# RWKV-5 attention into a SiLU layer pair: the loads, state copies and weight requests of the first eight units in another order

## The chip, the cores and the metric

The kernel runs on one core of one Trainium2 chip. A core has five engines with a queue each: TensorE (PE) for matrix products, VectorE (DVE), ScalarE (ACT) and GpSimd (POOL) for work on tiles, and SyncE (SP), which here only starts DMA transfers. ACT and POOL start transfers too. The engines run side by side and wait for each other by semaphores; within one queue the order is that of the program. The metric is device microseconds of one execution, as the median of five runs.

## The reference

The input of two matrix products with a SiLU between them is the output of a linear attention with a decaying state.

```python
batch, n_heads, seq, head_dim = (4, 8, 768, 48)
...
for t in range(S):
    cur = np.einsum('bhd,bhe->bhde', u[None] * kt, vt)
    y[:, :, t] = np.einsum('bhd,bhde->bhe', rt, state + cur)
    state = w[None, :, :, None] * state + np.einsum('bhd,bhe->bhde', kt, vt)
...
x = np.ascontiguousarray(attn_out.transpose(0, 2, 1, 3)).reshape(B * S, H * D)
h = x @ w_in          # 384 -> 2048
g = h * (1.0 / (1.0 + np.exp(-h)))
out = g @ w_out       # 2048 -> 384
```

r, k and v are fp32 of 4 x 8 x 768 x 48; the output is 3072 x 384.

## The kernel before

**Tiling.** The sequence is cut into six chunks of 128 steps. One chunk of one batch entry, all eight heads, is a *unit*; unit i has chunk i // 4 and batch entry i % 4, so there are 24. Units 0 to 3 are chunk 0 and have no earlier state.

**One unit** passes these steps; the two-letter words are those of the order string in the code.
- Loads `lr lk lv` of r, k, v (192 KB each, on SP's queue unless said otherwise; line 73).
- `T`: PE transposes r and k, in fp32, into one of two PSUM buffers called att (242). `rT kT`: DVE multiplies them by powers of the decay w, lamR and lamK (248). `A`: PE forms the 128 x 128 products of each head (270; for units from 4 on two units together, 283). `am`: DVE masks them to fp16 (290).
- The bonus term: `ku` (k times u, 202) and `ru` (times r, 206) on POOL, `rd`, a sum over the head's columns, on DVE (215), `vu` (that sum times v, 220) on POOL.
- `v16`: ACT casts v to fp16 (229; for odd units from 5 on two half copies more, 232 and 233). `r16`: ACT casts rT (263), needed when there is a state.
- `Y`: PE forms the outputs from am and v16, and from the state when there is one (300, 305). `y16`: DVE adds vu (333). `yT` and `xT`: PE transposes, ACT copies the result to the second layer's input (371, 375). From unit 6 on a DMA transposes instead (364).
- The state: `kc` (k times decay, POOL, 210), `S` (PE, 317), `sd` (old state times w to the 128th, POOL, 328), `st` (new state into SBUF, 344), `stb` (its fp16 copy, POOL, 353). In chunk 0 there is no old state, and `st` writes the fp16 copy (347) and the fp32 state (348) itself, each in two parts of 48 partitions.

**The layer pair.** `L` is a piece of the first product: two blocks of 128 hidden columns for two batch entries (386); `G` its SiLU on ACT (394). `L0.f` is for batch entries 0 and 1, `L2.f` for 2 and 3, f the first block. `H0` to `H3` do both for chunk 1. The second product is ops (407). The weights come in four parts each, `i_q0` to `i_q3` for w_in (84) and `i_o0` to `i_o3` for w_out (89), started from POOL and cast to fp16 on the way. Part n of w_in serves the blocks 4n to 4n + 3.

**PSUM.** y, yT, the state products, L's output and ops all take turns in one ring of four buffers with the tag `moe`; a new use waits until the use four turns earlier has been read.

**Order.** The work of units 0 to 5 and the first part of 6 and 7 is written out by hand in the order string: an instruction goes to the end of its engine's queue in the order of the words. `n*` ahead of a word puts n matmuls without use (`spin`, 157) on PE. After the string a loop handles two units at a time; pieces of the two layers are put between its steps by `fill`. In the loop's first turn (units 6 and 7) the bonus sums come behind both masks.

The setup ahead of the order string starts the loads of units 0 to 3, small loads of w and the load of u to all partitions (u_bc, 192 KB, line 105, on ACT's queue). v of unit 0 and k of unit 1 go by ACT's queue.

Of the kernel before, what the change touches and what calls it, by code (L numbers as in the profile page):

```python
# [15 lines left out]
def kernel(  # L16
# [11 lines left out]
    nc = tc.nc  # L28

    B, H, S, D = r.shape  # L30
    C = 128
    NCH = S // C
    HD = H * D
# [16 lines left out]
    def unit(i):  # L50
        return divmod(i, B)
# [10 lines left out]
    rin = [big.tile([128, H, 64], FP, name=f"rin{i}") for i in range(NIN)]  # L62
    kin = [big.tile([128, H, 64], FP, name=f"kin{i}") for i in range(NIN)]
    vin = [big.tile([128, H, D], FP, name=f"vin{i}") for i in range(NIN)]
    kc = [big.tile([128, H, 64], F16, name=f"kc{i}") for i in range(NIN)]
    st = [big.tile([PR, NP, PW], FP, name=f"st{b}") for b in range(B)]
    st16 = [big.tile([PR, NP, PW], F16, name=f"stb{b}") for b in range(B)]
# [3 lines left out]
    def ld(i, dst, src, eng=nc.sync):  # L71
        sc, b = unit(i)
        eng.dma_start(
            out=dst[i % NIN][:, :, 0:D],
            in_=src[b, :, sc * C:sc * C + C, :].rearrange("h t d -> t h d"))

    def load(i):
        if i >= NU:
            return
        for dst, src in ((rin, r), (kin, k), (vin, v)):  # L80
            ld(i, dst, src)
# [11 lines left out]
    def columns(eng, dst, src, j):  # L93
        eng.dma_start(out=dst[64 * j:64 * j + D, :],
                      in_=bass.AP(tensor=src.tensor, offset=D * j, ap=[[1, D], [PW, NP]]))

    w_row = cst.tile([1, HD], FP)
# [4 lines left out]
    nc.vector.memset(idle, 0.0)  # L102
    columns(nc.sync, wpT, w, 1)
    columns(nc.scalar, wpT, w, 0)
    nc.scalar.dma_start(out=u_bc, in_=bass.AP(tensor=u.tensor, offset=0,
                                              ap=[[0, 128], [D, H], [1, D]]))
    nc.scalar.dma_start(out=w_row, in_=bass.AP(tensor=w.tensor, offset=0, ap=[[0, 1], [1, HD]]))
    for i in range(B):
        for dst, src in ((rin, r), (kin, k), (vin, v)):
            by_act = (i == 0 and dst is vin) or (i == 1 and dst is kin)  # L110
            ld(i, dst, src, nc.scalar if by_act else nc.sync)
    nc.vector.memset(ones, 1.0)
    for i in range(B):
        nc.vector.memset(rin[i][:, :, D:64], 0.0)
# [1 line left out]
    for b in range(B):  # L116
# [13 lines left out]
        out=maskM, in_=maskM, compare_op=ALU.is_ge, fill=0.0,  # L130
# [10 lines left out]
    eK = cst.tile([PR, NP, C], FP)  # L141
    lamR = cst.tile([PR, NP, C], FP)
    lamK = cst.tile([PR, NP, C], FP)
    lnw_bc = cst.tile([128, HD], FP)
    lamC = cst.tile([128, H, D], FP)
# [47 lines left out]
    def L(i):  # L193
        return live.setdefault(i, {})

    def bonus_products(i):
        bonus_ku(i)
        bonus_rku(i)
# [10 lines left out]
    def decayed_k(i):  # L209
        nc.gpsimd.tensor_tensor(out=kc[i % NIN][:, :, 0:D], in0=kin[i % NIN][:, :, 0:D],  # L210
                                in1=lamC, op=ALU.mult)

    def bonus_sum(i):
        L(i)["rku"] = wrk.tile([128, H], FP, name="rku")
        nc.vector.tensor_reduce(out=L(i)["rku"], in_=L(i)["rku_f"],  # L215
                                axis=mybir.AxisListType.X, op=ALU.add)

    def bonus_v(i):
        L(i)["vu"] = wrk.tile([128, H, D], FP, name="vu")
        nc.gpsimd.tensor_tensor(out=L(i)["vu"], in0=vin[i % NIN],  # L220
                                in1=L(i)["rku"].unsqueeze(2).broadcast_to([128, H, D]),
                                op=ALU.mult)

    def crossed(i):
        return i >= B and i % 2 == 1
# [47 lines left out]
    def product_pair(i):  # L273
        a = [next_att().rearrange("p j (g c) -> p j g c", g=NP) for _ in range(2)]
        for e in range(2):
            L(i + e)["a"] = a[e]
        for s0, c0 in ((0, 0), (HC, HC)):
            for p in range(NP):
                for e in range(2):
                    rT, kT = L(i + e)["rT"], L(i + e)["kT"]  # L280
                    o0 = s0 if e == 0 else HC - s0
                    for j, r0 in ((0, 0), (1, 64)):
                        nc.tensor.matmul(a[e][o0:o0 + HC, j, p, c0:C],  # L283
                                         kT[r0:r0 + D, p, s0:s0 + HC],
                                         rT[r0:r0 + D, p, c0:C],
                                         start=True, stop=True)

    def masked(i):
        am = L(i)["am"] = wrk.tile([128, 2, NP, C], F16, name="am")
        nc.vector.tensor_tensor(  # L290
            out=am.rearrange("p h g c -> p (h g) c"), in0=L(i)["a"].rearrange("p h g c -> p (h g) c"),
            in1=(maskX if crossed(i) else maskM).unsqueeze(1).broadcast_to([128, H, C]), op=ALU.mult)
# [27 lines left out]
    def outputs(i):  # L320
        outputs_y(i)
        outputs_s(i)

    def decayed_state(i):
        sc, b = unit(i)
        if 0 < sc < NCH - 1:
            L(i)["sdec"] = wrk.tile([PR, NP, PW], FP, name="sdec", bufs=4)
            nc.gpsimd.tensor_tensor(out=L(i)["sdec"], in0=st[b],  # L328
                                    in1=wCT.unsqueeze(2).broadcast_to([PR, NP, PW]), op=ALU.mult)

    def evict_y(i):
        L(i)["y16"] = wrk.tile([128, H, D], F16, name="y16")
        nc.vector.tensor_tensor(out=L(i)["y16"], in0=L(i)["y"], in1=L(i)["vu"], op=ALU.add)  # L333

    def state(i):
        sc, b = unit(i)
        if sc == NCH - 1:
            return
        sps = L(i)["sps"]
        for p0, c0 in ((0, 0), (64, D)):  # L340
            dst = st[b][p0:p0 + D, :, c0:c0 + D]
            src = sps[p0:p0 + D, :, c0:c0 + D]
            if sc:
                nc.vector.tensor_tensor(out=dst, in0=src,
                                        in1=L(i)["sdec"][p0:p0 + D, :, c0:c0 + D], op=ALU.add)
            else:
                nc.scalar.copy(out=st16[b][p0:p0 + D, :, c0:c0 + D], in_=src)  # L347
                nc.scalar.copy(out=dst, in_=src)

    def state16(i):  # L350
        sc, b = unit(i)
# [74 lines left out]
    def fill(n):  # L426
        for _ in range(n):
            if fillers:
                fillers.pop(0)()
# [7 lines left out]
    def first(sc):  # L437
        return [lambda f=f: l1(sc, 0, B, f) for f in range(NFT)]
# [5 lines left out]
    def piece(word, f):  # L444
# [16 lines left out]
        "lr": lambda i: ld(i, rin, r), "lk": lambda i: ld(i, kin, k), "lv": lambda i: ld(i, vin, v),  # L461
    }
    order = """
        lnw eK lamK pads lr4 lk4 lv4 lr5 lk5 lv5 lr6 lk6 lv6 lr7 lk7 lv7 10*T0 ku0 kT0 rT0 v160
        ru0 5*A0 rd0 ku1 am0 T1 wb v161 ru1 lnwb lamC kT1 rT1 1*Y0 vu0 rd1 T2 i_q0 y160 A1 vu1
        yT0 xT0 v162 ku2 am1 kT2 rT2 ru2 4*Y1 y161 2*A2 yT1 xT1 i_q1 rd2 vu2 v163 T3 am2 ku3 kT3
        rT3 Y2 L0.0 y162 ru3 A3 i_q2 L0.2 G0.0 yT2 G0.2 xT2 rd3 am3 vu3 kc0 Y3 L0.4 G0.4 y163
        kc1 L0.6 G0.6 yT3 kc2 S0 st0 xT3 i_q3 kc3 L2.0 G2.0 L2.2 G2.2 S1 st1 L2.4 G2.4 L2.6 G2.6
        ku4 mx S2 st2 L0.8 G0.8 L0.10 G0.10 S3 st3 ru4 T4 kT4 rT4 v164 r164 L2.8 G2.8 L2.10
        G2.10 rd4 ku5 i_o0 vu4 T5 kT5 rT5 r165 v165 A45 ru5 kc4 sd4 L0.12 G0.12 am4 L0.14 G0.14  # L470
        am5 kc5 rd5 vu5 sd5 Y4 S4 y164 L2.12 G2.12 st4 Y5 S5 y165 L2.14 G2.14 st5 yT4 xT4 stb4
        stb5 i_o1 T6 kT6 rT6 yT5 xT5 ku6 ru6 i_o2 kc6 v166 r166 H0 H1 H2 T7 kT7 rT7 i_o3 H3 r167
        v167 ku7 ru7 kc7 sd6 sd7
    """
    for word in order.split():
        if "*" in word:
            n, word = word.split("*")
# [18 lines left out]
    for i in range(B + 2, NU, 2):  # L496
        sc, b = unit(i)
        nxt = range(i + 2, min(i + 4, NU))
        product_pair(i)
        if i > B + 2:  # L500
            for n in nxt:
                bonus_products(n)
                decayed_k(n)
        masked(i)
        masked(i + 1)
        if i == B + 2:
            for n in (i, i + 1):
                bonus_sum(n)
                bonus_v(n)
            for n in nxt:  # L510
                bonus_products(n)
                decayed_k(n)
        fill(4)
        outputs(i)
        evict_y(i)
        turn_y_dma(i)
        state(i)
        state16(i)
        fill(2)
        outputs(i + 1)  # L520
        evict_y(i + 1)
        turn_y_dma(i + 1)
        state(i + 1)
        state16(i + 1)
        if b:
            fillers.extend((first(sc) if sc > 1 else rest_first(sc)) + second(sc))
        fill(2)
        for n in nxt:
            turn(n)
            decay(n)  # L530
        load(i + B)
        load(i + 1 + B)
        for n in nxt:
            bonus_sum(n)
            cast_v(n)
            bonus_v(n)
            decayed_state(n)
        for n in nxt:
            fill(2)
            cast_r(n)  # L540
        fill(4)
# [31 lines left out]
```

## Time and profile before

| | |
|---|---|
| median of 5 runs | 197.89 us (197.85 to 198.14) |
| the profiled execution | 198.1 us, of which the span is 196.4 us |
| busy share of the span | PE 94%, weight loads 61%, DVE 50%, ACT 56%, POOL 61% |
| the chain that ended last | PE 76%, ACT 6%, DVE 6%, POOL 4%, DMA 4% |
| first product (386), PE | 384 matmuls, 67.7 us |
| second product (407), PE | 384 matmuls, 66.4 us |
| SiLU (394), ACT | 96 instructions, 55.4 us, mean 598 ns |
| `stb` and `st` of chunk 0 (347, 348), ACT | 16 instructions, 314 ns and 313 ns in the median |
| `ku`, `ru`, `kc` (202, 206, 210), POOL | 24 each, about 1000 ns each |
| `vu` (220), POOL | 24, 829 ns |
| w_in and w_out parts, request to landing | 6.3 and 5.7 us in the median |
| r, k, v, request to landing | 3.9, 3.8 and 4.0 us in the median |

The span is the time from the first instruction of the program to the last; the time of a run also holds what lies around it. Times within the span are told in us from its start. A share of busy time is an average over the whole span, which here has two parts: about 56 us in which the first units are worked off and the layer pair begins, and the rest, a regular loop.

### The profile page before, as it was taken

The page shows a single profiled execution, that of the slowest core. Times are in us where ns is not written, and L with a number is a line of the kernel's source. Part 1 is how long each engine was busy: PE and PEld are TensorE (multiplying, and loading weights), DVE is VectorE, ACT ScalarE, POOL GpSimd, SP SyncE. Part 2 cuts the span into 40 slices and gives each one's busy share as a digit, 9 for nine tenths or more (in the row PEclk, how much of TensorE's full clock was granted, in tenths as well). Part 3 has the DMA queues.
Part 4 walks back from the last instruction along what each step waited for, and adds up shares of the span by engine and source line. Part 5 has one row for each costly group of instructions (what it writes and reads, how often), then busy time and mean ns, then how long its engine had stood idle before and what let it go on. Part 6 is the DMA issues. An engine that isn't in the chain of part 4 may idle for free.

```text
span 196.4 us, 5505 instructions
## 1 busy us (share of the span) xinstructions
PE 183.8 (94%) x2250; PEld 120.3 (61%) x2250; DVE 97.9 (50%) x172; ACT 109.9 (56%) x223; POOL 120.4 (61%) x159
## 2 busy tenths in 40 slices
PE   7897868789989999999999999999999999999992
PEld 2465757667756787665556665556755657644561
DVE  6389503683682772782782673664564355100121
ACT  4672579968553286056794076792286781089200
POOL 8698993779999958919919829839739130000000
PEclk9999999999999999999999999999999999999998
DMA  4999999899939549259149268177286101410022
GB/s 73 249 181 207 216 201 171 157 191 128 133 78 193 173 84 197 92 125 218 38 84 216 67 152 193 23 142 163 74 183 150 40 3 40 120 43 0 0 80 80
DMA packets 90122, 24.33 MB, mean 124 GB/s; under 512 B 83313, under 2 KB 90098, under 8 KB 90098
## 3 DMA queue, kind: packets, MB, share of 16 engines
q1 hardware_dynamic: 83952, 20.26, 47.3%
q0 software_dynamic: 3712, 3.15, 11.5%
q10 hardware_dynamic: 2434, 0.59, 1.5%
q8 instruction: 17, 0.28, 0.6%
q14 instruction: 7, 0.06, 0.1%
HBM read 20.65 MB, written 4.72 MB: 129 GB/s over the span
## 4 chain that ended last, share of the span: by engine, by line
PE 76%; ACT 6%; DVE 6%; POOL 4%; DMA 4%; issue 2%; SPq 0%; POOLq 0%; DVEq 0%
PE ops L407 32%; PE hps L386 26%; PE att L283 6%; PE att L242 5%; PE att L270 2%; DVE am L290 2%; ACT gT L394 2%; DMA rin<-in_r_dram 2%; PE yp L305 2%; DMA vin<-in_v_dram 2%; PE yp L300 1%; PE sp L317 1%; DVE rT L248 1%; DVE kT L248 1%; ACT stb L347 1%
## 5 line engine op out<-in xcount | busy, mean ns | idle before, releaser
L386 PE MATMUL hps<-xT,win 128*128 128x256 f16 (+1 forms) x384 | 67.7, 326 | 3.0 <-ACT xT L375 2.4
L407 PE MATMUL ops<-wout,gT 128*128 128x384 f16 x384 | 66.4, 326 | 0.0
L394 ACT ACTIVATE gT<-hps 128x512 f16<-128x512 f32 x96 | 55.4, 598 | 18.2 <-PE hps L386 15.9
L386 PEld LDWEIGHTS <-win 128*128 128x128 f16 x384 | 35.8, 98 | 25.4 <-issue 3.2
L407 PEld LDWEIGHTS <-gT 128*128 128x128 f16 x384 | 36.2, 98 | 23.3
L220 POOL TENSOR_TENSOR vu<-vin,rku 128x384 f32<-128x384 f32 x24 | 19.8, 829 | 31.6 <-DVE rku L215 28.3
L413 ACT COPY osb<-ops 128x384 f32<-128x384 f32 x20 | 9.6, 480 | 45.1 <-PE ops L407 45.1
L290 DVE TENSOR_TENSOR am<-att,maskM 128x1024 f16<-128x1024 f32 x14 | 17.2, 1225 | 35.1 <-PE att L283 33.5
L202 POOL TENSOR_TENSOR ku<-kin,u_bc 128x384 f32<-128x384 f32 x24 | 24.1, 1003 | 1.8 <-DMA kin<-in_k_dram 1.6
L206 POOL TENSOR_TENSOR rku_f<-rin,ku 128x384 f32<-128x384 f32 x24 | 24.1, 1003 | 1.8
L210 POOL TENSOR_TENSOR kc<-kin,lamC 128x384 f16<-128x384 f32 x24 | 24.0, 1001 | 0.0
L248 DVE TENSOR_TENSOR kT<-att,lamK 112x512 f32<-112x512 f32 x24 | 16.4, 683 | 14.0 <-PE att L242 14.0
L333 DVE TENSOR_TENSOR y<-yp,vu 128x384 f16<-128x384 f32 x24 | 13.3, 556 | 14.9 <-POOL ku L202 4.5
L248 DVE TENSOR_TENSOR rT<-att,lamR 112x512 f32<-112x512 f32 x24 | 16.4, 685 | 7.2 <-ACT gT L394 4.0
L283 PE MATMUL att<-rT,kT 48*64 48x128 f32 (+1 forms) x640 | 16.5, 248 | 1.3 <-DVE rT L248 1.3
L283 PEld LDWEIGHTS att<-rT,kT 48*64 48x64 f32 x640 | 14.7, 133 | 4.9 <-issue 3.1
L415 DVE COPY osb<-ops 128x384 f32<-128x384 f32 x4 | 2.2, 558 | 22.4 <-PE ops L407 22.4
L328 POOL TENSOR_TENSOR sdec<-st,wCT 112x384 f32<-112x384 f32 x16 | 13.2, 827 | 0.0
L229 ACT CAST v<-vin 128x384 f16<-128x384 f32 x24 | 11.5, 512 | 2.2 <-DMA vin<-in_v_dram 2.1
L263 ACT CAST rT<-rT 112x512 f16<-112x512 f32 x20 | 12.5, 623 | 0.4 <-DVE rT L248 0.3
L215 DVE TENSOR_REDUCE rku<-rku_f 128x8 f32<-128x384 f32 x24 | 12.3, 544 | 0.1
L290 DVE TENSOR_TENSOR am<-att,maskX 128x1024 f16<-128x1024 f32 x10 | 12.2, 1215 | 0.0
(60 smaller groups left out, 168.6 us busy)
## 6 DMA issues: line engine op xcount, KB each, us to landing
rin<-in_r_dram SPq DMA_DIRECT2D x24, 192.0 KB, 3.9
out_dram<-osb SPq DMA_DIRECT2D x24, 192.0 KB, 2.1
kin<-in_k_dram SPq DMA_DIRECT2D x23, 192.0 KB, 3.8
vin<-in_v_dram SPq DMA_DIRECT2D x23, 192.0 KB, 4.0
win<-in_moe_w_in_dram POOLq DMA_DIRECT2D x4, 384.0 KB, 6.3
wout<-in_moe_w_out_dram POOLq DMA_DIRECT2D x4, 384.0 KB, 5.7
xT<-y SPq DMA_TRANSPOSE x18, 2.3
u_bc<-in_u_dram ACTq DMA_DIRECT2D x1, 192.0 KB, 4.0
```

The costliest lines, as they stand in the source:

```text
L202: nc.gpsimd.tensor_tensor(out=L(i)["ku"], in0=kin[i % NIN][:, :, 0:D], in1=u_bc, op=ALU.mult)
L206: nc.gpsimd.tensor_tensor(out=L(i)["rku_f"], in0=rin[i % NIN][:, :, 0:D], in1=L(i)["ku"], op=ALU.mult)
L210: nc.gpsimd.tensor_tensor(out=kc[i % NIN][:, :, 0:D], in0=kin[i % NIN][:, :, 0:D], in1=lamC, op=ALU.mult)
L220: nc.gpsimd.tensor_tensor(out=L(i)["vu"], in0=vin[i % NIN], in1=L(i)["rku"].unsqueeze(2).broadcast_to([128, H, D]), op=ALU.mult)
L248: nc.vector.tensor_tensor(out=L(i)[key].rearrange("p g (y t) -> p y g t", y=2), in0=L(i)["t"][0:PR, :, x], in1=lam.rearrange("p g (y t) -> ...
L283: nc.tensor.matmul(a[e][o0:o0 + HC, j, p, c0:C], kT[r0:r0 + D, p, s0:s0 + HC], rT[r0:r0 + D, p, c0:C], start=True, stop=True)
L290: nc.vector.tensor_tensor(out=am.rearrange("p h g c -> p (h g) c"), in0=L(i)["a"].rearrange("p h g c -> p (h g) c"), in1=(maskX if crossed ...
L328: nc.gpsimd.tensor_tensor(out=L(i)["sdec"], in0=st[b], in1=wCT.unsqueeze(2).broadcast_to([PR, NP, PW]), op=ALU.mult)
L333: nc.vector.tensor_tensor(out=L(i)["y16"], in0=L(i)["y"], in1=L(i)["vu"], op=ALU.add)
L386: nc.tensor.matmul(hps[:, f, :], win[:, q, (ft + f) * 128:(ft + f + 1) * 128], xts[sc][:, q, b0:b0 + nb, :].rearrange("p b t -> p (b t)"), ...
L394: nc.scalar.activation(out=gts[sc][:, ft:ft + m, b0 * C:(b0 + nb) * C], in_=hpss[b0, ft], func=AF.Silu)
L407: nc.tensor.matmul(opss[b], gts[sc][:, ft, b * C:(b + 1) * C], wout[:, ft, :], start=(ft == 0), stop=(ft == NFT - 1))
```

## The change

The change has four parts, all in the first eight units.

1. **Setup.** r of unit 0 goes first on SP's queue, and k of unit 0 goes on ACT's queue ahead of u_bc; v of unit 0 and all loads of units 1 to 3 go on SP's queue.
2. **State copies.** The sixteen copies of chunk 0's state products out of PSUM are DVE's and no longer ACT's.
3. **The order string.** 18 spin matmuls instead of 22; rT0 ahead of kT0; vu0 and i_q0 ahead of ru1; rd1 behind am1; T4, kT4, rT4, mx and kc3 earlier; the pieces L2 and L0 mixed otherwise; T5 before L2.10. i_q3 now stands behind ku4 and ru4, i_o0 behind ru5, i_o1 and i_o2 behind ku6 and ru6, i_o3 behind ku7. H0 to H3 stand between the steps of units 6 and 7; stb4 and stb5 come last. kc6, kc7, sd6 and sd7 leave the string and go into the loop's first turn.
4. **The loop's first turn.** For units 6 and 7 the order is vu6 kc6 sd6, am6, rd7, am7, vu7 kc7 sd7 (rd6 is the last but two of the string).

```diff
-    nc.scalar.dma_start(out=u_bc, in_=bass.AP(tensor=u.tensor, offset=0,
-                                              ap=[[0, 128], [D, H], [1, D]]))
     nc.scalar.dma_start(out=w_row, in_=bass.AP(tensor=w.tensor, offset=0, ap=[[0, 1], [1, HD]]))
-    for i in range(B):
-        for dst, src in ((rin, r), (kin, k), (vin, v)):
-            by_act = (i == 0 and dst is vin) or (i == 1 and dst is kin)
-            ld(i, dst, src, nc.scalar if by_act else nc.sync)
+    ld(0, rin, r)
+    ld(0, kin, k, nc.scalar)
+    nc.scalar.dma_start(out=u_bc, in_=bass.AP(tensor=u.tensor, offset=0,
+                                              ap=[[0, 128], [D, H], [1, D]]))
+    ld(0, vin, v)
+    for i in range(1, B):
+        load(i)
...
-                nc.scalar.copy(out=st16[b][p0:p0 + D, :, c0:c0 + D], in_=src)
-                nc.scalar.copy(out=dst, in_=src)
+                nc.vector.tensor_copy(out=st16[b][p0:p0 + D, :, c0:c0 + D], in_=src)
+                nc.vector.tensor_copy(out=dst, in_=src)
...
     order = """
-        lnw eK lamK pads lr4 lk4 lv4 lr5 lk5 lv5 lr6 lk6 lv6 lr7 lk7 lv7 10*T0 ku0 kT0 rT0 v160
-        ru0 5*A0 rd0 ku1 am0 T1 wb v161 ru1 lnwb lamC kT1 rT1 1*Y0 vu0 rd1 T2 i_q0 y160 A1 vu1
-        yT0 xT0 v162 ku2 am1 kT2 rT2 ru2 4*Y1 y161 2*A2 yT1 xT1 i_q1 rd2 vu2 v163 T3 am2 ku3 kT3
+        lnw eK lamK pads lr4 lk4 lv4 lr5 lk5 lv5 lr6 lk6 lv6 lr7 lk7 lv7 8*T0 ku0 rT0 kT0 v160
+        ru0 3*A0 rd0 ku1 am0 T1 wb v161 vu0 lnwb lamC i_q0 kT1 rT1 1*Y0 ru1 T2 y160 A1 yT0 xT0
+        v162 ku2 am1 rd1 vu1 kT2 rT2 ru2 4*Y1 y161 2*A2 yT1 xT1 i_q1 rd2 vu2 v163 T3 am2 ku3 kT3
         rT3 Y2 L0.0 y162 ru3 A3 i_q2 L0.2 G0.0 yT2 G0.2 xT2 rd3 am3 vu3 kc0 Y3 L0.4 G0.4 y163
-        kc1 L0.6 G0.6 yT3 kc2 S0 st0 xT3 i_q3 kc3 L2.0 G2.0 L2.2 G2.2 S1 st1 L2.4 G2.4 L2.6 G2.6
-        ku4 mx S2 st2 L0.8 G0.8 L0.10 G0.10 S3 st3 ru4 T4 kT4 rT4 v164 r164 L2.8 G2.8 L2.10
-        G2.10 rd4 ku5 i_o0 vu4 T5 kT5 rT5 r165 v165 A45 ru5 kc4 sd4 L0.12 G0.12 am4 L0.14 G0.14
-        am5 kc5 rd5 vu5 sd5 Y4 S4 y164 L2.12 G2.12 st4 Y5 S5 y165 L2.14 G2.14 st5 yT4 xT4 stb4
-        stb5 i_o1 T6 kT6 rT6 yT5 xT5 ku6 ru6 i_o2 kc6 v166 r166 H0 H1 H2 T7 kT7 rT7 i_o3 H3 r167
-        v167 ku7 ru7 kc7 sd6 sd7
+        kc1 L0.6 G0.6 yT3 xT3 mx S0 st0 kc2 T4 kT4 rT4 kc3 L2.0 G2.0 S1 L2.2 G2.2 st1 ku4 v164
+        L2.4 G2.4 S2 L2.6 G2.6 st2 ru4 i_q3 r164 L0.8 G0.8 S3 L0.10 G0.10 st3 rd4 ku5 L2.8 G2.8
+        T5 kT5 rT5 L2.10 G2.10 vu4 ru5 i_o0 A45 rd5 am4 r165 v165 L0.12 G0.12 vu5 kc4 L0.14
+        G0.14 am5 L2.12 G2.12 sd4 kc5 Y4 S4 y164 st4 L2.14 G2.14 sd5 Y5 S5 yT4 xT4 y165 st5 yT5
+        xT5 H0 T6 kT6 rT6 ku6 ru6 i_o1 i_o2 H1 v166 r166 H2 H3 T7 kT7 rT7 ku7 i_o3 v167 r167 ru7
+        rd6 stb4 stb5
     """
...
-        masked(i)
-        masked(i + 1)
-        if i == B + 2:
-            for n in (i, i + 1):
-                bonus_sum(n)
-                bonus_v(n)
+        if i > B + 2:
+            masked(i)
+            masked(i + 1)
+        else:
+            bonus_v(i)
+            decayed_k(i)
+            decayed_state(i)
+            masked(i)
+            bonus_sum(i + 1)
+            masked(i + 1)
+            bonus_v(i + 1)
+            decayed_k(i + 1)
+            decayed_state(i + 1)
             for n in nxt:
                 bonus_products(n)
                 decayed_k(n)
```

## The prediction

> **What bounds the kernel now.** I read the page's 40 slices first, then busy time by stage, then the chain of waits, then who waits for whom in the stage that the change rewrites.
>
> ```profile
> PE   7897868789989999999999999999999999999992
> ACT  4672579968553286056794076792286781089200
> POOL 8698993779999958919919829839739130000000
> ```
>
> A slice is 4.9 us. TensorE (PE) is full from the twelfth slice to the end and has holes only before. The busy time by stage (stretch, its length, then busy us of PE, weight loads, DVE, ACT, POOL) puts a number on it:
>
> ```profile
> 22.40:35.60 13.20, 9.78 (x123) 8.26 (x123) 3.59 (x6) 11.32 (x32) 9.74 (x12) 1.00 1.16 195
> 35.60:46.50 10.90, 10.00 (x178) 8.52 (x178) 7.07 (x13) 8.30 (x17) 8.19 (x11) 1.00 0.86 154
> 46.50:56.20 9.70, 8.59 (x139) 6.67 (x138) 6.11 (x12) 5.01 (x9) 9.50 (x12) 1.00 0.80 112
> 56.20:172.00 115.80, 115.80 (x1506) 74.67 (x1506) 62.67 (x105) 63.84 (x123) 74.29 (x89) 1.00 0.54 120
> ```
>
> From 56.20 (PE begins the transposes of unit 8) PE is never idle, and the chain of waits stays on it to 192.9. The instructions behind that point are the same in both programs and keep their order on PE. So the end moves by as much as this point moves; I call it T8. It is reached at 56.16. Between 22.4 and 56.2 PE idles (13.20 - 9.78) + (10.90 - 10.00) + (9.70 - 8.59) = 5.4 us; that is about the most the order string can give there.
>
> Two queues make those holes, as the chain of waits (start, us, what) and then the timeline (with the idle time before an instruction and who ended it) show:
>
> ```profile
> 24.71 0.20 ACT stb L347
> 24.91 0.21 ACT st L348
> 25.13 0.32 ACT stb L347
> 25.45 0.22 ACT st L348
> 25.69 0.49 ACT xT L375
> ...
> 53.17 0.80 POOL vu L220
> 53.99 0.57 DVE y L333
> 54.60 0.33 PE sp L317 x4
> 54.93 1.30 PE ops L407 x8
> ```
>
> ```profile
> 32.16 1.47 PE L386 MATMUL hps<-xT,win 128*128 128x256 f16 x12 [0.60 <-ACT st L348]
> ...
> 31.60 0.69 DVE L248 TENSOR_TENSOR kT<-att,lamK 112x512 f32<-112x512 f32 x1 [8.17 <-PE att L242]
> 33.44 0.82 POOL L220 TENSOR_TENSOR vu<-vin,rku 128x384 f32<-128x384 f32 x1 [3.36 <-DVE rku L215]
> ```
>
> From 24 to 36 us it is ACT: the state copies stand between the SiLUs and the xT copy, PE waits behind them, and DVE meanwhile sits idle for 8.17 us. From 43 to 54 it is POOL: it lost 3.36 and 2.17 us earlier waiting for bonus sums, and now `stb4 stb5`, three weight requests, `ku kc sd` of units 6 and 7 stand before `vu6 vu7`, for which y6 and then S7 wait (0.85 us of PE).
>
> **The start (r0, k0 on two queues): priced at nothing by unit 2.** r0 lands at 5.85 and T0 starts at 5.99, k0 follows at 6.6. The trace shows u_bc's 1536-byte packets sharing the engines with r0 from 3.0 to 5.0, while r0 trickles at a quarter of the rate that 192-byte packets reach at 5.0. *Trainium skill, "DMA: Bandwidth & Descriptors", "Issuing engines are not separate DMA queues"*: queues share the same 16 engines, and a second issuer saves only sequencer time. By that rule alone two queues save the 0.47 us between the issues of r0 (1.43) and k0 (1.90). By the row the gain is larger, because u_bc steps behind k0: at the observed 340 packets per 0.25 us, 2048 packets need 1.5 us, so both land near 5.0 and A0 starts 1.3 us earlier (7.5 instead of 8.85). But u_bc now lands near 6.8, and `ku0` needs it: ku0 6.9, ru0 7.9 to 8.9 (1.0 us rows), rd0 0.55, and rd0 stands before am0 on DVE: am0 at 9.45, not 10.06. Then the new order has rd1 behind am1 (0.5 us on DVE in front of kT2; `vu0 i_q0` now precede `ru1` on POOL). kT2 comes at 14.9; in the trace 14.88. On the fair assumption that u_bc needs the same 2 us as before, A2, am3 and Y3 stay where they are (Y3 22.4 to 22.5), and POOL is 0.5 us later at `vu3`. Bounds: u_bc at 6.2 gives -0.6, at 8.0 gives +1.0. The four spin matmuls that go (18 instead of 22) lay inside waits for r0 and rT0: eight end at 4.9, still just ahead of T0, and three end before A0. ACT issues one load fewer ahead of `lnw` (3.69, directly behind k1's issue), so the powers are early; SP passes the same loads in another order.
>
> **State copies to DVE.** Removed from ACT: 16 copies, 314 ns by row, 0.20 to 0.32 us start to start, 1.05 us per unit, 4.2 us in all, in a stage where ACT is busy 11.32 of 13.20. Added to DVE: 16 copies of 48x192 out of PSUM. Nearest row: `st<-sp,sdec` 48x192 on DVE, 355 ns (L344); back-to-back DVE rows start 0.08 us sooner than their duration says (kT 0.68, rT 0.60 behind it). I take 0.30 us each, ends 0.25 and 0.36, 1.2 us per unit. *Trainium skill, "VectorE: DVE Perf Modes", the errata section's cycle table* speaks against the move: from PSUM, (120+192)/0.96 = 325 ns on VectorE against (172+192)/1.2 = 303 on ScalarE. By the rule the move costs 22 ns a copy; by the row 41. Either is small beside freeing 4.2 us of the queue that PE waits for, as long as DVE's idle 8.17 us takes it.
>
> **The walk from Y3 to T8**, with durations from the rows: a two-block SiLU step L 0.65 us of PE, its G starts 0.85 behind L's start and takes 0.60 (0.55 back to back), T 0.6, pair product 1.5, am 1.23, xT 0.48, POOL 1.0 for ku, ru, kc and 0.8 for vu, sd and each request. The PSUM tag `moe` has four buffers, so each user waits for the fourth before it.
> - win1 is requested at 16.9 (15.84 before) and needs 6.1: L0.4 at 23.0. Then L0.6, yT3, S0 at 24.5; xT3 25.1 to 25.6; L2.0 25.6, S1, L2.2, L2.4, S2 to 28.0.
> - DVE: st0 24.9 to 26.1, kT4 and rT4 to 27.3, st1 to 28.4. L2.6 needs S1's buffer: 28.45 (a new PE hole of 0.5). Then L0.8, S3, L0.10, L2.8, T5 from 31.35; st3 ends 31.4, rd4 31.9, kT5 and rT5 to 33.3.
> - **A45 33.35 to 34.85**; in the trace 35.60 to 37.15. Gain so far 2.3.
> - POOL: kc3 26, ku4 27, ru4 28; win3 requested at 28.0 (24.50 before), landing 34.3 at its median 6.3: just before L0.12 at 34.85. vu4 waits for rd4: 31.95. ru5, wout0 33.8, vu5, kc4 36.4, sd4, kc5, sd5 39.0, ku6, ru6 41.0, wout1 41.0, wout2 41.8, ku7, wout3 43.6, ru7, stb4, stb5 46.4, vu6 47.2, kc6, sd6, vu7 49.9. Before, vu7 ended at 54.7.
> - L0.12, L0.14, L2.12, Y4 36.8, L2.14, Y5, S5, yT4, yT5 39.4; ACT ends xT5 at 40.0 (r165, three v casts and four G lie before it), H0 40.05; 43.13 before. H1 to H3, T7 43.25, rT7 45.2, A67 to 46.8, four fillers to 49.4, Y6, 8 ops, Y7, S7 without the 0.85 wait, 8 ops: **T8 at 53.2**.
>
> Of the other moves, `mx` (two ACT copies, 0.6 us) now lies ahead of G2.0, hidden by T4 and L2.0 on PE; rd7 between am6 and am7 costs DVE 0.5 us while PE has 2.6 us of fillers and Y6; H0 to H3 only change places with S, Y and T. `vu kc sd` of units 6 and 7 go from one block to two, the same six instructions.
>
> Sum: 56.16 - 53.2 = 3.0 us. r8 and k8 for T8 are on SP ahead of the last three weights, as before (landed by 44 there). POOL begins ku8 1.5 us ahead of T8 in both, so the steady part keeps its cover. If DVE's cover is gone, the price is the second rival below.
>
> Against the profiled execution: 198.1, span 196.4, 1.7 around it. 196.4 - 3.0 + 1.7 = 195.1; it ran 0.2 above the median of 197.89, so **194.9**. Unknowns of the likeliest case: start -0.6 to +1.0, copies -0.4 to +0.5, small waits that I missed. Its own range: 194.1 to 195.9.
>
> **Rivals.**
> - *Weights late* (0.20). win3 now leaves behind unit 4's products, wout3 behind `ku7`. Other loads took up to 9.1 us in this stage when SP's rows were in front; with that, win3 lands at 37.1, L0.12 stands 2.2 us, of which about 0.5 comes back where H0 waits for ACT. Or wout3, third of a train whose landings stand 2.7 us apart (48.36, 51.01, 53.81 in the trace), lands at 51.7, needed at 52.5; one us more and T8 waits. Gain 0.7 to 2, in the middle 1.4: 196.5. For: request and need stand only 0.6 and 0.8 us apart. Against: with fewer requests before 28 us the stream is emptier.
> - *The copies hold DVE, and DVE holds POOL* (0.11; slower). rd4 stands behind all 16 copies and vu4 behind rd4; behind vu4 stand wout0 to wout3 in POOL's order. T8 is at least vu4 + 20.5 (11.7 of POOL to wout3, 8.1 to land, 0.7 of PE). vu4 may be 35.7 before that passes 56.2, so copies of over 0.53 us each turn it. At 0.556, the row of y (128x384 out of PSUM), T8 is 56.6: 198.3; with u_bc late as well 199.3. Against: these copies have half the columns, and the 355 ns row is the same shape.
> - *Nothing* (0.05): gain and late weights cancel, 197.9.
> - *More* (0.06): u_bc early and no hole at L2.6: 193.5. It cannot pass 5.4 us plus the start's 0.6.
>
> The likeliest case has 0.58. No change means within 0.2% (0.4 us), about what a measurement of this kernel tells apart. Faster: 0.58 + 0.06 + 0.20 = 0.84; same 0.05; slower 0.11. Eight in ten lie between 193.8 and 197.3: the likeliest case, the late weights and most of the larger gain.
>
> **What will show it.** T0 near 5.0 but am0 near 9.5 and kT2 near 14.9 (start worth nothing). DVE rows `stb`, `st` near 0.33 us and no 8 us idle on DVE. A45 at 33 to 34; xT5's end at 40; POOL's second vu of units 6 and 7 ended by 50; T8 at 53. Wrong, if L0.12 waits for win, ops for wout, or POOL's vu4 comes after 34.

## The result and the profile after

| | before | after |
|---|---|---|
| median of all runs | 197.98 us (197.85 to 200.37, 47 runs) | 197.19 us (195.33 to 199.76, 28 runs) |
| ratio, 95% interval | | 0.9937 (0.9921 to 0.9954) |
| profiled execution, its span | 198.1, 196.4 us | 197.95, 196.2 us |
| T8 (PE begins unit 8) in it | 56.16 | 56.02 |
| Y3 in it | 22.39 | 24.55 |
| Y3 to T8 | 33.77 | 31.47 |

The kernel became faster by 0.6%, about 1.25 us (197.98 x 0.0063); 3.0 were forecast. The ratio is of the fast runs alone, whose means are 196.93 and 198.18 us (four of the changed kernel's 28 are slow ones), while the medians of all runs differ by 0.79. The profiled execution gained only 0.15, and its two halves went opposite ways: the stretch from Y3 to T8 got 2.30 us shorter, and Y3 came 2.16 us later. Y3 and T8 on PE's timeline (start, duration, what, count, and in brackets the idle time before it), each before and then after:

```profile
22.39 0.37 PE L305 MATMUL yp<-v,am 128*128 128x48 f16 x8 [0.40 <-DVE am L290]
24.55 0.37 PE L306 MATMUL yp<-v,am 128*128 128x48 f16 x8 [0.40 <-DVE am L291]
...
56.16 0.43 PE L242 MATMUL att<-ident,rin 64*112 64x64 f32 x8
56.02 0.44 PE L243 MATMUL att<-ident,rin 64*112 64x64 f32 x8
```

The page's slices of the changed kernel show both; the row PEclk is the clock that PE was granted, in tenths of full speed, and the last line is that row of the kernel before:

```profile
PE   7789789987999999999999999999999999999992
ACT  5561469768553285056793076791286781089200
POOL 8486994999999948919919829839738330000000
PEclk9975999999999999999999999999999999999999
...
PEclk9999999999999999999999999999999999999998
```

PE's digits are 9 from the eleventh slice on, against the thirteenth before (T8 lies in the twelfth, which has an 8). But the clock row, which showed only 9s in the first 56 us of the kernel before, has a 7 and a 5 in the third and fourth slice, 9.8 to 19.6 us. The busy time by stage (stretch, its length, busy us of PE, weight loads, DVE, ACT, POOL, then the granted clock) shows that these two slices are one stretch at exactly half clock:

```profile
5.25:12.08 6.83, 4.89 (x74) 3.14 (x72) 3.73 (x6) 4.35 (x15) 4.47 (x5) 1.00 1.04 207
12.08:18.91 6.83, 6.72 (x51) 4.36 (x49) 4.80 (x8) 1.71 (x3) 4.54 (x6) 0.50 0.98 177
22.40:35.60 13.20, 11.68 (x148) 9.55 (x144) 10.15 (x25) 8.71 (x18) 9.68 (x12) 1.00 1.07 189
24.55:56.02 31.47, 28.28 (x438) 23.23 (x439) 22.05 (x45) 20.99 (x41) 27.80 (x33) 1.00 1.01 169
```

In the stretch 22.40 to 35.60, where PE was busy 9.78 us before, it is busy 11.68 now, DVE 10.15 instead of 3.59 and ACT 8.71 instead of 11.32: that is the part that was meant to be gained. PE's timeline shows what half clock means, and what came ahead of it:

```profile
5.89 0.44 PE L243 MATMUL att<-ident,kin 64*112 64x64 f32 x8 [0.46 <-DMA kin<-in_k_dram]
6.27 0.82 PE L158 MATMUL zs<-idle 128*128 128x512 f16 x3
7.79 1.16 PE L271 MATMUL att<-rT,kT 48*128 48x128 f32 x16 [0.70 <-DVE kT L249]
...
10.20 0.39 PE L158 MATMUL zs<-idle 128*128 128x512 f16 x1
11.38 0.37 PE L306 MATMUL yp<-v,am 128*128 128x48 f16 x8 [0.79 <-DVE am L291]
...
12.58 2.08 PE L271 MATMUL att<-rT,kT 48*128 48x128 f32 x16
...
14.88 1.91 PE L158 MATMUL zs<-idle 128*128 128x512 f16 x4
```

Before, the same stretch was this:

```profile
5.99 0.68 PE L242 MATMUL att<-ident,rin 64*112 64x64 f32 x8 [0.25 <-DMA rin<-in_r_dram]
7.33 1.25 PE L157 MATMUL zs<-idle 128*128 128x512 f16 x5
8.85 1.16 PE L270 MATMUL att<-rT,kT 48*128 48x128 f32 x16 [0.27 <-DVE rT L248]
...
13.80 1.03 PE L157 MATMUL zs<-idle 128*128 128x512 f16 x4
```

The products A of unit 1 take 2.08 us where those of unit 0 took 1.16, and four spin matmuls 1.91 us where the same four took 1.03 before. The holes ahead of it, 0.46, 0.70 and 0.79 us, are short. The one of 0.70 stands where the change took spin matmuls away; the one of 0.79 where PE's work came earlier and `am0`, for which it waits, did not.

Because A of unit 1 is late, `am1`, `rd1` and `vu1` are late, and on POOL the request of the second part of w_in stands behind `vu1` and `ru2`. It leaves at 18.20 where 16.9 was forecast:

```profile
16.47 0.83 POOL L221 TENSOR_TENSOR vu<-vin,rku 128x384 f32<-128x384 f32 x1 [2.27 <-DVE rku L216]
17.25 1.01 POOL L207 TENSOR_TENSOR rku_f<-rin,ku 128x384 f32<-128x384 f32 x1
18.20 0.80 POOL L84 DMA_DIRECT2D win<-in_moe_w_in_dram  x1
```

```profile
25.65 1.49 PE L387 MATMUL hps<-xT,win 128*128 128x256 f16 x12 [0.73 <-DMA win<-in_moe_w_in_dram]
```

PE waits 0.73 us for it at L0.4, inside the stretch that was to be gained. So this loss, too, begins in the start.

**The theory** from here: the walk from Y3 to T8 does what was forecast, and the start, priced at nothing, loses TensorE's clock, because the spin matmuls that are gone had kept PE busy. **Rivals:** the start is slow for another reason (loads in the new order, bonus sums behind the mask); the copies on DVE or the late weight requests cost part of the gain.

### The profile page after: what moved, and what is told of

It is laid out like the page before. It is cut to its first block, busy times and chain, and to the rows that moved or that the text cites. A ratio compares the mean times of both kernels' runs of the same rounds, so it can differ in the third digit from the quotient of the medians.

```text
span 196.2 us, 5495 instructions
## 1 busy us (share of the span) xinstructions
PE 185.2 (94%) x2246; PEld 121.3 (62%) x2246; DVE 102.9 (52%) x188; ACT 106.1 (54%) x207; POOL 120.2 (61%) x159
## 4 chain that ended last, share of the span: by engine, by line
PE 80%; DMA 6%; POOL 3%; DVE 3%; issue 2%; ACT 2%; ACTq 0%; POOLq 0%; DVEq 0%
PE ops L408 32%; PE hps L387 30%; PE att L284 8%; PE att L243 5%; DMA win<-in_moe_w_in_dram 4%; DMA u_bc<-in_u_dram 3%; PE yp L306 2%; PE yp L301 2%; PE sp L318 2%; POOL ku L203 1%; POOL rku_f L207 1%; ACT gT L395 1%; POOL vu L221 1%; DVE rT L249 1%; DVE st L349 1%
## 5 line engine op out<-in xcount | busy, mean ns | idle before, releaser
L395 ACT ACTIVATE gT<-hps 128x512 f16<-128x512 f32 x96 | 56.0, 598 | 21.1 <-PE hps L387 18.6
L387 PEld LDWEIGHTS <-win 128*128 128x128 f16 x384 | 35.7, 98 | 24.0 <-issue 0.9
L221 POOL TENSOR_TENSOR vu<-vin,rku 128x384 f32<-128x384 f32 x24 | 19.8, 829 | 30.7 <-DVE rku L216 27.4
L416 DVE COPY osb<-ops 128x384 f32<-128x384 f32 x4 | 2.2, 558 | 22.4 <-PE ops L408 22.4
L306 PEld LDWEIGHTS <-am 128*128 128x128 f16 x192 | 10.0, 98 | 4.2 <-DVE am L291 2.5
```

The lines of the kernel that those rows point to most:

```text
L221: nc.gpsimd.tensor_tensor(out=L(i)["vu"], in0=vin[i % NIN], in1=L(i)["rku"].unsqueeze(2).broadcast_to([128, H, D]), op=ALU.mult)
L306: nc.tensor.matmul(L(i)["y"][:, h, :], L(i)["am"][:, j, p, :], L(i)["vy"][:, h, :], start=not sc, stop=(not sc or j == 1))
L387: nc.tensor.matmul(hps[:, f, :], win[:, q, (ft + f) * 128:(ft + f + 1) * 128], xts[sc][:, q, b0:b0 + nb, :].rearrange("p b t -> p (b t)"), ...
L395: nc.scalar.activation(out=gts[sc][:, ft:ft + m, b0 * C:(b0 + nb) * C], in_=hpss[b0, ft], func=AF.Silu)
```

## The experiments

The kernel before ran beside each group: 198.48 us in the median beside the first four (197.96 to 199.51; about half of those executions took 199.2 to 199.5), 198.24 beside the next four, 197.91 beside the last four. Ratios are to it; where the groups are compared with each other, I give us as well. The upper half of the first group's neighbour makes the ratios of e1 to e4 up to 0.3% lower than they would be against its lower half, of about 198.2.

### The start and the rest apart

`e3_old_start` has the setup and the order string up to rT3 of the kernel before (with its 22 spins), and everything behind it of the changed kernel. `e4_new_start_only` is the reverse: the new setup and order up to rT3, the old copies, the old order behind it and the old first turn of the loop.

```diff
-        ... 8*T0 ku0 rT0 kT0 v160
-        ru0 3*A0 rd0 ku1 am0 T1 wb v161 vu0 lnwb lamC i_q0 kT1 rT1 1*Y0 ru1 T2 y160 A1 yT0 xT0
-        v162 ku2 am1 rd1 vu1 kT2 rT2 ru2 4*Y1 y161 2*A2 ...
+        ... 10*T0 ku0 kT0 rT0 v160
+        ru0 5*A0 rd0 ku1 am0 T1 wb v161 ru1 lnwb lamC kT1 rT1 1*Y0 vu0 rd1 T2 i_q0 y160 A1 vu1
+        yT0 xT0 v162 ku2 am1 kT2 rT2 ru2 4*Y1 y161 2*A2 ...
```

> The loads, the spins and the order up to rT3 as before; from Y2 on all as in the change (copies on VectorE, late weights, the loop's first turn). Theory C, and my walk with a start worth nothing: Y3 at 22.4, the clock stays whole, T8 at 53.5 to 54.2, ratio 0.987 to 0.990. Theory D with the loss in the late weights of the middle part: the start is not to blame, ratio 0.993 to 0.995 as in the whole change.

> The loads, the spins and the order up to rT3 of the change; from Y2 on all as before. Theory C: slower than before by what the low clock costs, on the mean 1 to 1.5 us, ratio 1.004 to 1.008, with executions at full clock at 1.000. Theory D (the start is neutral, as I priced it): ratio 0.999 to 1.002.

| | old rest | new rest |
|---|---|---|
| old start | 197.98 (beside these: 198.48) | 195.61 (194.82 to 196.5), 0.9846 (0.9808 to 0.9885) |
| new start | 199.87 (198.32 to 201.37), 1.0042 (1.0012 to 1.0073) | 197.19, 0.9937 (0.9921 to 0.9954) |

The rest gains 2.4 to 2.9 us with the old start (195.61 against 197.98 or 198.48) and 2.7 with the new one. The new start alone costs 1.4 to 1.9 with the old rest, 1.6 with the new one. By the ratios, each with its neighbour, the rest gains 1.5%, the start costs 0.4% (0.8 us), and both together gain 0.6%, so the two do not add up exactly. In kind both readings agree: the rest is worth nearly what was forecast, and the start ate much of it. The stretches of e4 on either side of the fall show the same fall of the clock, without a single one of the moved copies and with the later weight requests as they were before:

```profile
4.71:11.54 6.83, 5.04 (x61) 2.94 (x61) 3.17 (x5) 3.87 (x14) 4.35 (x8) 1.00 0.93 193
11.54:14.95 3.41, 3.41 (x44) 3.12 (x42) 1.68 (x4) 1.85 (x3) 2.66 (x3) 0.50 0.97 179
```

In e3's profile the start is that of the kernel before, instruction for instruction, and yet full clock comes at 10.14 us (7.25 before). Y3 is at 23.64, where 22.4 was expected, and T8 at 54.21, at the end of the 53.5 to 54.2 expected. When the clock comes is not settled by the instructions alone.

### Spins added to the changed kernel, taken from the one before

`e1_more_spin` fills the two larger holes of the changed kernel. `e2_before_few_spins` gives the kernel before the spin counts of the changed one and changes nothing else.

```diff
-        ru0 3*A0 rd0 ku1 am0 T1 wb v161 vu0 lnwb lamC i_q0 kT1 rT1 1*Y0 ru1 T2 y160 A1 yT0 xT0
+        ru0 6*A0 rd0 ku1 am0 T1 wb v161 vu0 lnwb lamC i_q0 kT1 rT1 5*Y0 ru1 T2 y160 A1 yT0 xT0
```

```diff
-        ... 10*T0 ku0 kT0 rT0 v160
-        ru0 5*A0 rd0 ku1 ...
+        ... 8*T0 ku0 kT0 rT0 v160
+        ru0 3*A0 rd0 ku1 ...
```

> The changed kernel with seven spin matmuls more: six instead of three ahead of A0 and five instead of one ahead of Y0, the two places where PE stood for 0.70 and 0.79 us in its trace. Theory C (the clock gate: thinner work on PE in the first 12 us lets the granted clock fall to half for 6.8 us, which costs about 2 us in those executions): the low stretch goes, the clock row shows no 5 in slices 2 to 5, kT3 comes at 18.5 instead of 20.7, and the median falls from 196.7 to 195.2 to 195.8, ratio to before 0.987 to 0.990. Theory D (dependencies: u_bc at 7.4, rd0 ahead of am0, rd1 behind am1, win1 late): spins in waits change nothing, 196.5 to 197.2.

> The kernel before with the spin counts of the change (8 ahead of T0, 3 ahead of A0) and nothing else. Theory C: the waits of PE in the first 9 us grow by about 1.7 us, the clock falls in some executions there too, and the median rises by 0.5 to 2 us with a wider spread, ratio 1.003 to 1.010. Theory D: these spins lay in waits, ratio 0.999 to 1.001.

e1: 195.78 us (195.64 to 198.67), 0.9861 (0.9826 to 0.9895): 1.4 us less than the 197.19 of the changed kernel, 0.9 less than its six later executions (g0, 196.65). In its profile the clock is full from 4.49 us to the end of PE's work. The stages of its profile, the second of them its own way from Y3 to T8:

```profile
5.25:12.08 6.83, 6.18 (x75) 3.77 (x77) 3.77 (x6) 4.40 (x15) 4.51 (x5) 1.00 1.04 205
22.86:53.71 30.85, 28.27 (x437) 23.20 (x437) 22.05 (x45) 20.99 (x41) 28.17 (x33) 1.00 1.04 178
```

In the stretch where PE of the changed kernel was busy 4.89 us it is busy 6.18; with that nothing falls. On PE's timeline the five spins now end as am0 is ready, and A of unit 1 takes its 1.16 us again:

```profile
10.18 1.25 PE L158 MATMUL zs<-idle 128*128 128x512 f16 x5
11.34 0.37 PE L306 MATMUL yp<-v,am 128*128 128x48 f16 x8
...
12.54 1.16 PE L271 MATMUL att<-rT,kT 48*128 48x128 f32 x16 [0.23 <-DVE rT L249]
```

e2: 201.74 us (201.51 to 201.86), 1.0152 (1.0122 to 1.0182). Four spins fewer, and nothing else, cost the kernel before 3 us. That is more than the 1.003 to 1.010 expected, and the wider spread that was expected did not come. PE's timeline of e2:

```profile
6.27 0.67 PE L242 MATMUL att<-ident,rin 64*112 64x64 f32 x8 [1.39 <-DMA rin<-in_r_dram]
...
9.15 2.08 PE L270 MATMUL att<-rT,kT 48*128 48x128 f32 x16
...
15.34 2.02 PE L270 MATMUL att<-rT,kT 48*128 48x128 f32 x16
```

The spins now end 1.39 us ahead of T0 (0.25 before; 0.28 of the difference is r0, which here landed later), and both products are still slow: full clock comes only at 17.46 us, against 7.25 before. So the clock is not lost again here, as was expected, but comes late. The clock row of this run's page says 9 all the same, because the first change that the profiler recorded is that at 17.46. At the start the clock is read from durations of like instructions, 2.08 against 1.16 us. For the same reason a recorded mean clock says little: four of e2's six executions have 0.972 to 0.974 and two 1.00, this profile among them, and all take the same time.

### Which of the two holes

`g1_hole_before_A0` has only the three spins ahead of A0 more, `g2_hole_before_Y0` only the four ahead of Y0; `g0_after_again` is the changed kernel beside them. `g3_before_more_spins` gives the kernel before three and four more at the same places.

```diff
-        ru0 5*A0 rd0 ku1 am0 T1 wb v161 ru1 lnwb lamC kT1 rT1 1*Y0 vu0 rd1 T2 i_q0 y160 A1 vu1
+        ru0 8*A0 rd0 ku1 am0 T1 wb v161 ru1 lnwb lamC kT1 rT1 5*Y0 vu0 rd1 T2 i_q0 y160 A1 vu1
```

> The changed kernel unedited, on the chip of the next three, so that they can be compared with it. Expected 0.994 of before as in the first result; in its profile the granted clock falls to half for one or two stretches of 3.4 us between 8 and 20 us, or comes late.

> Three spin matmuls more ahead of A0 alone (21 in all). If the clock is lost through the hole ahead of A0 that the change tore, this alone gives what seven gave: 0.986 of before, full clock throughout. If it is the sum of PE's holes in the first 12 us that counts, this fills about half of it: 0.988 to 0.992, the half-clock stretch only in some executions. If the spins are worth nothing, 0.994 as the changed kernel beside it.

> Four spin matmuls more ahead of Y0 alone (22 in all, as many as before, in another place). If the hole ahead of A0 is the one that counts: 0.994. If the sum of the holes counts: 0.987 to 0.992. If only the number of spins counts: 0.986.

> The kernel before with three spins more ahead of A0 and four more ahead of Y0 (29 in all). If spins pay only by keeping the granted clock, which before has from 7.25 us on anyway, this stays within 0.3% of before (0.997 to 1.002). If they pay in another way, it gains what they gave the changed kernel, 0.8% (0.992).

| | us | ratio |
|---|---|---|
| g0, the changed kernel | 196.65 (195.33 to 197.55) | 0.9932 (0.9907 to 0.9956) |
| g1, A0 only | 196.66 (195.89 to 197.82) | 0.9940 (0.9918 to 0.9963) |
| g2, Y0 only | 196.49 (196.34 to 200.76) | 0.9931 (0.9919 to 0.9944) |
| g3, before with seven more | 198.78 (198.67 to 200.8) | 1.0059 (1.0032 to 1.0086) |

One hole filled is worth nothing measurable; with both filled, e1 (195.78 us, 0.9826 to 0.9895) and f2 below (195.51 us, 0.9830 to 0.9900, on the same chip as these four) lie outside these intervals. So the hole ahead of A0 alone is not what counts. The sum of the holes missed too: g1 should have come to 0.988 to 0.992, and it came to 0.994. Only in kind does g1 fit: of its six executions four had a mean granted clock of 0.982 to 0.991, as 16 of the changed kernel's 28 have, two had 1.00, and the profile of one of those (span 194.2, the hole of 0.69 us ahead of Y0 still in it) is as good as that of e1. g2's profile caught its longest execution, 200.76 us, in which k0 came late, full clock came at 16.43 and fell once more, so it says little of the others. Why those take some 196.4 with a recorded clock of 0.997 to 1.00 is open; a late first grant would leave such a record, as in e2, but no trace of them shows it.

g3 missed too: 0.997 to 1.002 was expected from the clock, and it is slower by 0.6%. The rival that spins pay in some other way predicted a gain and is refuted, and the spins' own price is seen. PE's timeline of the kernel before, then of g3:

```profile
11.23 0.39 PE L157 MATMUL zs<-idle 128*128 128x512 f16 x1
11.46 0.36 PE L305 MATMUL yp<-v,am 128*128 128x48 f16 x8
```

```profile
11.39 1.25 PE L157 MATMUL zs<-idle 128*128 128x512 f16 x5
12.48 0.36 PE L305 MATMUL yp<-v,am 128*128 128x48 f16 x8
```

Before, PE had no wait at Y0 that four more spins could fill: Y0 comes 1.02 us later (0.16 of it from the three more ahead of A0), Y3 0.69 later (23.08), T8 0.68 (56.84). In the changed kernel the same four fill a wait of 0.79 us.

### Copies and weights

Both start from e1, whose clock holds. `f1_copies_on_act` puts the sixteen copies back on ACT; `f2_weights_early` puts `i_q3` behind kc2, `i_o0` behind ku5 and `i_o1` ahead of ku6.

```diff
-                nc.vector.tensor_copy(out=st16[b][p0:p0 + D, :, c0:c0 + D], in_=src)
-                nc.vector.tensor_copy(out=dst, in_=src)
+                nc.scalar.copy(out=st16[b][p0:p0 + D, :, c0:c0 + D], in_=src)
+                nc.scalar.copy(out=dst, in_=src)
```

```diff
-        ... kc2 T4 ... ru4 i_q3 r164 ... ku5 L2.8 ... ru5 i_o0 A45 ... ku6 ru6 i_o1 i_o2 ...
+        ... kc2 i_q3 T4 ... ru4 r164 ... ku5 i_o0 L2.8 ... ru5 A45 ... i_o1 ku6 ru6 i_o2 ...
```

> The change with seven spin matmuls more (as in the first experiment, 195.8) and the sixteen state copies of chunk 0 back on ScalarE, nothing else. The prediction's step: ACT is busy 8.1 of the 12.6 us from 22.4 to 35.0 in the changed kernel; 4.2 us more fill it, xT3, G2.0 and the r casts come late, am4 at 36 to 37.5 instead of 35.1, T8 1 to 2.3 us later, 196.8 to 198.1. Rival: the new order gives the gain by itself and ACT has slack: 195.6 to 196.3.

> The change with seven spin matmuls more, and win3 requested behind kc2 (not behind ku4 and ru4), wout0 behind ku5 (not behind ru5), wout1 ahead of ku6. The prediction priced the late requests at nothing: 195.5 to 196.2, win3 landing near 32 instead of 34 to 35. Rival (the late requests are what lets the rows of units 4 to 6 land in time): rows of units 5 and 6 land 2 us later, T5 or T6 waits, 196.5 to 197.5. Other rival (late weights cost): faster, below 195.3.

f1: 197.2 us (196.63 to 199.66), 0.9948 (0.9918 to 0.9979), so the copies on DVE are worth 1.4 us (against e1) to 1.7 (against f2). In its profile Y3 to T8 takes 32.13 us, 1.28 more than in e1. DVE's timeline of the changed kernel and ACT's of f1 show the copies of units 0 and 1:

```profile
27.50 0.35 DVE L348 CAST stb<-sp 48x192 f16<-48x192 f32 x1 [1.92 <-PE sp L318]
27.78 0.34 DVE L349 COPY st<-sp 48x192 f32<-48x192 f32 x1
28.15 0.36 DVE L348 CAST stb<-sp 48x192 f16<-48x192 f32 x1
28.43 0.35 DVE L349 COPY st<-sp 48x192 f32<-48x192 f32 x1
```

```profile
27.14 0.31 ACT L348 CAST stb<-sp 48x192 f16<-48x192 f32 x1
27.36 0.31 ACT L349 COPY st<-sp 48x192 f32<-48x192 f32 x1
27.70 1.08 ACT L395 ACTIVATE gT<-hps 128x512 f16<-128x512 f32 x2
28.67 0.30 ACT L348 CAST stb<-sp 48x192 f16<-48x192 f32 x1
```

On DVE each copy costs some 0.04 us more (0.34 to 0.36 against 0.30 to 0.31), but it falls where DVE sat idle for 8.17 us before. On ACT the four copies of a unit stand between SiLUs, and in f1 PE waits for a SiLU twice (0.34 and 0.16 us), which in e1 it does not. The rest of the 1.28 us is not assigned to single waits.

f2: 195.51 us (195.25 to 196.98), 0.9865 (0.9830 to 0.9900), the same as e1. The fourth part of w_in landed at 30.81 instead of just before its need, and nothing came of it that shows: within intervals of some 0.35% to either side, the late requests neither gain nor cost.

### The loads by themselves

`f4_new_loads_old_order` has the new setup with the old order string up to rT3 (8, 6 and 5 spins ahead of T0, A0, Y0); `f5_old_start_spin` the old setup with the same order and 12, 6 and 3 spins. Behind rT3 both are the changed kernel.

```diff
-        ... 8*T0 ku0 kT0 rT0 v160
-        ru0 6*A0 rd0 ku1 am0 T1 wb v161 ru1 lnwb lamC kT1 rT1 5*Y0 ...
+        ... 12*T0 ku0 kT0 rT0 v160
+        ru0 6*A0 rd0 ku1 am0 T1 wb v161 ru1 lnwb lamC kT1 rT1 3*Y0 ...
```

> The loads of the change, the order of the kernel before up to rT3 (kT0 ahead of rT0, ru1 ahead of vu0, rd1 ahead of am1) with 8 spins ahead of T0, 6 ahead of A0, 5 ahead of Y0; the rest as the change. If rd1 behind am1 costs what I priced (0.5 us on DVE ahead of kT2), kT2 comes at 14.9 instead of 15.35, Y3 at 22.4, and the median is 195.2 to 195.5. If ru1 is held up by rd0 and u_bc so that rd1 makes am1 late, no gain: 195.6 to 196.2.

> The start as before with 12 instead of 10 spins ahead of T0, 6 instead of 5 ahead of A0, 3 instead of 1 ahead of Y0; the rest as the change. In the run with the old start r0 came at 6.4, PE stood for 0.74 us at 5.7 and the full clock came only at 10.1 us, Y3 at 23.6. Theory C: without that hole the full clock comes at 4 to 7.5 us in every execution, Y3 at 22.3 to 22.8, median 194.7 to 195.1 with a spread under 0.5. Rival (the onset only follows the phase of the window): as before the addition, 194.8 to 196.5.

f4: 195.23 us (194.74 to 196.46), 0.9843 (0.9805 to 0.9881). f5: 195.46 us (195.0 to 196.8), 0.9859 (0.9823 to 0.9894). f4 came as expected in its median and in kT2 (14.80), but its Y3 is at 22.85, not 22.4. f5 missed: had a filled hole settled the clock, 194.7 to 195.1 with a spread under 0.5 was expected; it came to 195.46 with a spread of 1.8. Its profile does show what was expected (full clock at 5.59, Y3 at 22.48), but not every execution can be like it. The rival, by which such spins do not settle when the clock comes, fits (194.8 to 196.5). The order of the loads makes no difference that shows, once PE is kept busy. Both beat the kernel before and the changed one by intervals that do not touch; f4, f5, f2, e1 and e3 are not told apart from each other. The best of them is about 1.5% faster than before, where the change as it was made brought 0.6%.

## Why the prediction was wrong, by its own steps

**The sign and the mechanism held, the size did not.** A gain of 3.0 us was forecast (194.9 us), and 1.25 came (a median of 197.19). The wide range (193.8 to 197.3) holds the time by luck, since it was widened for late weights, which is not what happened; the likeliest case's own range (194.1 to 195.9) does not hold it.

- **What failed: the sentence on the spins,** "The four spin matmuls that go (18 instead of 22) lay inside waits for r0 and rT0", priced at nothing. It took a spin for an instruction that costs or saves only its own time on PE's queue. e2 took just those four from the kernel before and lost 3 us; e1 gave the changed kernel seven and gained 0.9 to 1.4. How few would do, and in which places, is open: g1 and g2 did not find it. In the profiled execution T8 came 2.82 us later than the walk had it (56.02 against 53.2). The account, with e1 as the same kernel at full clock: Y3 came at 24.55, in e1 at 22.86, so 1.69 is the clock; 0.62 more comes behind Y3 (31.47 - 30.85), where L0.4 waits for the late second part of w_in; the rest, 0.51, is late in e1 too.
- **The rest of the start: bounds right, end wrong.** r0 landed at 4.47 and k0 at 5.76 ("both near 5.0" was forecast), u_bc at 7.38 instead of 6.8. From 3.75 to 5.0 us the trace has some 570 packets of v0, next on SP's queue, beside those of k0; the walk had left v0 out. `am0` starts at 10.11, no earlier than before (10.06; 9.45 forecast), and with `rd1` behind `am1` kT2 comes at 15.35 in e1 (14.88 before, 14.9 forecast). Y3 is 0.47 later than before in e1: inside -0.6 to +1.0, but not nothing. k0 came 0.84 us earlier, between what the rule of one set of engines gave (0.47) and what the row gave (1.6); r0 came 1.38 earlier, more than either; u_bc paid for it.
- **The walk from Y3 to T8 was right.** Forecast 53.2 - 22.45 = 30.7 us; measured 30.85 in e1, 30.57 and 30.58 in e3 and f5. In e1, with Y3 0.4 late: vu4 32.24 (31.95 forecast), A45 33.54 (33.35), xT5's end 40.29 (40.0), vu7's end 49.99 (49.9), T8 53.71 (53.2). The 1.02 us that A67 waits for rT7 are in the walk (T7 at 43.25, rT7 at 45.2). It counted a hole of 0.5 at L2.6 that does not show; 0.18 at L0.8 does. And it counted no wait at L0.4, where PE waited 0.49 us in f2 and 0.27 in f4, at full clock.
- **The copies:** 0.30 us each was taken. On DVE the four of a unit start 0.28 to 0.37 apart, 1.32 us from the first to kT4 behind the fourth, where 1.2 was counted; rows of 0.34 to 0.36. DVE's idle took them, as supposed.
- **Weights late** (0.20): did not happen. L0.12 waits for nothing, ops wait for nothing, and f2 shows that earlier requests gain nothing. The part that was late is another one, the second of w_in. The clock made most of that: requested at 18.20 in the changed kernel and at 17.23 in e1, where 16.9 was forecast. But in f2, at full clock and requested at 17.08, it still held L0.4 for 0.49 us.
- **The copies hold DVE, and DVE holds POOL** (0.11): vu4 came at 32.24 in e1, far from the 35.7 from which it decides. Even with the late start of the changed kernel's profile it came at 34.54, still 1.2 ahead of that.

The walk looked at every instruction behind 22 us and gave the first 22 one paragraph. There the profile of before had the warning in plain sight: the ten spins from 1.29 us on start 0.43 us apart, the five from 7.33 on 0.22 apart (five in 1.25). PE's clock came on between them, in the very stretch from which the change takes spins.

## What to carry to other kernels

A matmul without use may be paying for the clock: before one is removed, or a hole is opened beside it, compare durations of like instructions ahead of it and behind it, and price the removal by what half clock would cost the work that follows. It pays only where PE waits anyway: in g3, where PE had little to wait for, seven of them moved T8 by 0.68 us. When several edits go together, run the parts crossed (old and new start, old and new rest): two runs here showed that one part won about 2.7 us and the other gave back about 1.6.

## What the runs showed of the hardware

The fall of the clock follows no long pause. *The Trainium skill, "TensorE: Matmul & The Clock Gate", "HAM oscillation — how this bites in real kernels"*, gives the rule of no PE-idle gap above some 3.4 us; by that rule alone the clock would have stayed, but here the longest gap between the grant and the fall was 0.79 us (0.84 in g2), and the measurement decides. Every fall in the profiles ended a stretch of full clock of exactly 6.83 us that began with the first grant. None came later, until PE's work was over: from 24.31 to 27.72 PE was busy for only 47% before (1.61 of 3.41 us), and the clock stayed full. The stretches between two changes of the clock, up to the first change behind PE's last matmul, are all whole multiples of 3.41 us, from 3.41 to 191.15. PE's busy share in the two halves of the first 6.83 us after the grant, worked out from all fourteen profiles (the six others are before, e1, e3, f2, f5 and g1):

```
                   first 3.41 us   second 3.41 us   then
after                   0.66            0.77        half for 6.83 us
g0                      0.74            0.76        half for 3.41 us
e4                      0.74            0.73        half for 3.41 us
g2                      0.94            0.62        half for 3.41 us
f1                      0.73            0.88        full
f4                      0.69            1.00        full
g3                      0.70            1.00        full
e2                      0.85            0.82        full
six others         0.77 to 1.00    0.87 to 1.00     full
```

All four that fell had the second half below 0.78, and all ten that held had it above 0.81; the first half doesn't sort them. That was found behind the runs and no run was made to test it, so it is an observation and not a rule. The moment of the first grant also varies, from 4.07 us (g1) to 17.46 (e2) after the span's start, and it does so where the start is the same in every instruction: 7.25 before and 10.14 in e3, 5.25 in the changed kernel and 6.14 in g0. That this is also what spreads the changed kernel's executions over 195.33 to 199.76 us is likely but not shown, since only profiled executions have a trace.
